# One order table for attention, RMS norm and channel mix on one core: the planner replaced, 1/rms in one pass

## The chip, the cores and the metric

The kernel runs on one core of a Trainium2 chip. Its time is the device time of one execution in microseconds; the median of several runs counts. Five engines work side by side, each through its own queue in order: TensorE (PE; its weight loads are shown apart as PEld), VectorE (DVE), ScalarE (ACT), GpSimd (POOL) and SyncE (SP). PE writes its results to PSUM, and DVE or ACT bring them to SBUF. POOL issues the loads here, SP the stores.

## What is computed

```python
# q, k, v: (8, 8, 576, 64)
kv  = einsum('bhsd,bhse->bhde', k, v)
out = einsum('bhsd,bhde->bhse', q, kv)
out = out / sqrt(mean(out * out, axis=-1) + 1e-6) * g_norm
x   = out.transpose(0, 2, 1, 3).reshape(8, 576, 512)
xp  = x shifted by one token within each batch, zero first
xk  = mu_k * x + (1 - mu_k) * xp
xr  = mu_r * x + (1 - mu_r) * xp
kk  = max(xk @ w_k, 0)                 # w_k 512 x 1024
y   = (kk * kk) @ w_v                  # w_v 1024 x 512
return sigmoid(xr @ w_r) * y           # w_r 512 x 512
```

Inputs are float32; the loads turn them into bfloat16, and the result is stored in float32.

## The kernel before

**Two halves of the work.** Attention goes by batch b (0 to 7, 576 tokens each), the channel mix by group g (0 to 8, 512 tokens each). Group g needs all batches that its tokens lie in: group 0 batch 0, group 1 batches 0 and 1, group 2 batches 1 and 2, and so on. The blended inputs lie in two rings, `xk` and `xr`, of four batches.

**Tokens and heads.** Eight heads make four head pairs (hp), and two head pairs make one z (z is 0 or 1). Features lie on the partitions and tokens on the free side. Token 9p + j stands in column 64j + p, so the shift by one token is a shift by 64 columns, with a small wrap at the edge.

**The pieces of one batch**, with their lines: `kv` (L354, 72 small matmuls) and its copy kc; `q`, the transposes of q (L362, 36 for one z), and the copy qc; `u`, which is q times kv (L369), and the copy uc (L222 on ACT, L224 on DVE); `sq`, the square on DVE (L579, L423 in batch 0); `ss`, the sum over a head by a matrix of ones (L591, L428), which leaves the sum on every partition; the logarithm of the mean plus eps on ACT (L595, L435) and the exponential of minus half of it (L599, L439), which is 1/rms; `mul`, u times 1/rms into xT on DVE (L613, L442); `wr`, the wrap (L614, L506); `d`, the difference of a token and the one before (L624, L465); `mk` and `mr`, d times a column of mu_k or mu_r, one instruction for each head pair (L638, L471); and `xk` and `xr`, that plus the token before (L641, L473). In batch 0 all of it goes in two parts of the tokens, a and b, so that group 0 can start early, and its last 64 tokens (w) come later, for group 1.

**The pieces of one group**: `k` (L692, L491 and L710 in group 0), eight pieces of four matmuls with 512 columns; `relu` on ACT (L696), one for two pieces; `ksq`, its square on DVE (L699, L716); `r`, four pieces of four (L740), and `sig` on ACT (L745); `v`, eight pieces of four (L761, L778 in the last group); `out`, v times sig on DVE (L765, L785); and the stores (L674). That makes 80 matmuls of 512 columns for a group.

**The order.** Each piece is put into a list with a set of engines that it can run on, its price, its dependencies, its buffers and a due time. `Planner.run` then plays the list through with prices of its own, takes at each step the piece that can start earliest (within a window of 0.04 us the one with the earliest due time, which counts attention from `T0 + TG * (b - 2)` and groups from `T0 + TG * g`), gives it to an engine, and emits all pieces in that order. Engines run in the order of emission. An "idle" piece of 128-column matmuls on zeros (L661) is put where PE would wait, up to a piece of batch 0.

**Buffers.** Rings hold a few tiles for each name: two each for `mm` (k, r, v) and `at` (kv, q, u, ss) in PSUM, where a tile is two banks; three for k, v and q of one batch. `qT`, `uT`, `xT`, `md` have two tiles of four head pairs, `sq`, `rs` and `d` one.

**Loads** are issued on POOL: batch 0 in pieces of 288 KB by z, then w_k in two halves of rows, w_r, w_v in one piece of 1024 KB, then each batch in three of 576 KB (q of batch 1 in two). g_norm is folded into w_k and w_r by a scaling with a column (L318). ACT changes its function table between logarithm with exponential and sigmoid (L231).

## Time and profile before

| | |
|---|---|
| median of 3 runs | 222.52 us (222.42 to 223.12) |
| the profiled execution's own time | 222.89 us |
| its span, first to last instruction | 221.1 us |
| mean granted PE clock | 0.985 |
| PE busy | 201.7 us, of which 12.7 on zeros |
| DVE, ACT, POOL busy | 145.8, 134.2, 24.2 us |
| table loads on ACT | 14, 18.0 us |
| loads and stores | 26.57 MB moved, mean 120 GB/s |

The span leaves out what lies before the first instruction and behind the last, 1.8 us here. Busy time of PE is not PE at its peak: matmuls are pipelined, so the mean of one (357 to 382 ns with 512 columns) is longer than its share of a run of them (16 take 3.45 us). A row of the groups gives line, engine, operation, output and input with shapes, count, then busy us, mean ns of one, and the idle time of the engine ahead of it with what ended it.

### The profile page before, as it was taken

Reading aid. Unit: us, or ns where it says so; the run is one execution under the profiler, and the core shown is the slowest. Engines: PE = TensorE matmul, PEld = TensorE weight load, DVE = VectorE, ACT = ScalarE, POOL = GpSimd, SP = SyncE. Lnnn points to the kernel's source line nnn. Section 1 sums busy time; section 2 is a strip of 40 time slices with the busy share of each in tenths; the row PEclk is TensorE's granted clock in tenths of the full one; section 3 lists DMA queues with packets and bytes.
Section 4 is the critical chain, followed back from the end, with each engine's and each line's share of the span. In section 5 each row is a group of like instructions: output and inputs, shape, how many; then the busy total and the mean of one; then the engine's idle time right before and its main releaser. Section 6 shows DMA issues by size and latency. Waiting matters only on the chain.

```text
span 221.1 us, 5309 instructions
## 1 busy us (share of the span) xinstructions
PE 201.7 (91%) x2260; PEld 108.0 (49%) x2285; DVE 145.8 (66%) x292; ACT 134.2 (61%) x171; POOL 24.2 (11%) x37
## 2 busy tenths in 40 slices
PE   8858779964999999999999999999999999999992
PEld 7746554443444544444345764453444444444451
DVE  1139995769995699969947993899299524224231
ACT  2236554685769987993898489749965704603610
POOL 7732124121210021000000000000000000000000
PEclk9999999996799999999999999999999999999999
DMA  5999999999999999815102500340044026007024
GB/s 81 180 210 204 208 208 207 208 241 256 206 208 208 208 233 234 150 40 128 26 0 66 127 2 3 82 110 0 3 95 96 0 47 145 0 12 181 0 68 125
DMA packets 20812, 26.57 MB, mean 120 GB/s; under 512 B 1708, under 2 KB 15796, under 8 KB 20788
## 3 DMA queue, kind: packets, MB, share of 16 engines
q0 software_dynamic: 14848, 16.78, 45.0%
q1 hardware_dynamic: 5540, 8.92, 16.2%
q10 hardware_dynamic: 400, 0.52, 0.7%
q8 instruction: 18, 0.29, 0.5%
q14 instruction: 6, 0.05, 0.1%
HBM read 33.56 MB, written 9.44 MB: 194 GB/s over the span
## 4 chain that ended last, share of the span: by engine, by line
PE 72%; DVE 10%; ACT 7%; DMA 4%; issue 4%; POOL 1%; POOLq 0%; DVEq 0%
PE mm L761 22%; PE mm L692 22%; PE mm L740 14%; DMA v<-in_v_dram 4%; PE at L591 2%; PE at L369 2%; PE at L362 2%; PE at L354 2%; PE at L778 2%; PE mm L778 2%; PE mm L710 2%; ACT relu L696 1%; DVE out L765 1%; ACT ln L595 1%; ACT uT L222 1%
## 5 line engine op out<-in xcount | busy, mean ns | idle before, releaser
L692 PE MATMUL mm<-xk,w_k 128*128 128x512 bf16 (+1 forms) x274 | 59.8, 357 | 1.2 <-issue 0.9
L696 ACT ACTIVATE relu<-mm 128x1024 bf16<-128x1024 f32 x36 | 36.8, 1025 | 39.1 <-PE mm L692 34.5
L761 PE MATMUL mm<-w_v,sqk 128*128 128x512 bf16 x248 | 57.6, 379 | 0.5 <-issue 0.2
L765 DVE TENSOR_TENSOR out<-mm,sig 128x1024 f32<-128x1024 f32 x16 | 19.6, 1223 | 33.5 <-ACT ln L595 15.4
L692 PEld LDWEIGHTS <-w_k 128*128 128x128 bf16 x288 | 26.2, 98 | 25.2 <-issue 1.1
L761 PEld LDWEIGHTS <-sqk 128*128 128x128 bf16 x256 | 24.6, 98 | 27.4 <-issue 0.5
L740 PE MATMUL mm<-w_r,xr 128*128 128x512 bf16 x141 | 32.4, 379 | 1.4 <-ACT relu L696 1.1
L699 DVE TENSOR_TENSOR sqk<-relu 128x1024 bf16<-128x1024 bf16 x32 | 21.9, 686 | 9.3 <-ACT relu L696 9.2
L740 PEld LDWEIGHTS <-xr 128*128 128x128 bf16 x144 | 13.6, 98 | 17.4 <-DVE w_r L318 1.4
L745 ACT ACTIVATE sig<-mm 128x1024 bf16<-128x1024 f32 x18 | 18.4, 1025 | 5.9 <-PE mm L740 5.7
L595 ACT ACTIVATE ln<-at,eps 128x576 f32<-128x576 f32 x28 | 19.2, 741 | 0.3 <-PE at L591 0.3
L638 DVE TENSOR_SCALAR md<-d,cols 128x576 bf16<-128x576 bf16 x56 | 18.5, 373 | 0.3
L231 ACT ACT_TABLE_LOAD x14 | 18.0, 1283 | 1.0 <-PEq L826 0.7
L599 ACT ACTIVATE rs<-ln 128x576 bf16<-128x576 f32 x28 | 17.7, 689 | 0.0
L222 ACT CAST uT<-at 128x576 bf16<-128x576 f32 (+2 forms) x24 | 13.4, 595 | 5.2 <-PE at L369 5.0
L224 DVE COPY qT<-at 128x1152 bf16<-128x1152 bf16 (+2 forms) x12 | 8.2, 682 | 10.2 <-PE at L362 10.1
L661 PE MATMUL mm<-zero 128*128 128x128 bf16 x147 | 12.7, 249 | 1.1 <-DVE zero L258 1.1
L222 ACT CAST kv<-at 128x256 bf16<-128x256 f32 (+1 forms) x9 | 3.2, 352 | 17.2 <-PE at L354 17.2
L579 DVE TENSOR_TENSOR sq<-uT 128x1152 bf16<-128x1152 bf16 x14 | 10.5, 754 | 2.9 <-PE at L591 2.5
L369 PE MATMUL at<-qT,kv 64*64 64x288 bf16 (+2 forms) x128 | 10.2, 321 | 2.0 <-ACT qT L222 1.0
L661 PEld LDWEIGHTS <-zero 128*128 128x128 bf16 x147 | 10.8, 114 | 1.9 <-DVE zero L258 1.1
L641 DVE TENSOR_TENSOR xr<-md,xT 128x1152 bf16<-128x1152 bf16 x14 | 10.6, 759 | 0.5
(58 smaller groups left out, 179.3 us busy)
## 6 DMA issues: line engine op xcount, KB each, us to landing
out_dram<-out SPq DMA_DIRECT2D x67, 128.0 KB, 2.4
k<-in_k_dram POOLq DMA_DIRECT2D x7, 576.0 KB, 20.2
v<-in_v_dram POOLq DMA_DIRECT2D x7, 576.0 KB, 21.6
q<-in_q_dram POOLq DMA_DIRECT2D x6, 576.0 KB, 21.6
q<-in_q_dram POOLq DMA_DIRECT2D x4, 288.0 KB, 15.0
w_k<-in_moe_w_k_dram POOLq DMA_DIRECT2D x2, 512.0 KB, 12.5
w_v<-in_moe_w_v_dram POOLq DMA_DIRECT2D x1, 1024.0 KB, 19.3
k<-in_k_dram POOLq DMA_DIRECT2D x2, 288.0 KB, 5.7
```

Source lines behind the costliest of these rows:

```text
L222: nc.scalar.copy(out=dst, in_=src)
L231: nc.scalar.preload_act_table_set(name)
L595: nc.scalar.activation(out=get(ln)[:, :, 0:HS], in_=ps.t[:, :, 0:HS], func=AF.Ln, bias=eps, scale=1.0 / HD)
L638: nc.vector.tensor_scalar(out=get(md)[:, hp], in0=d.t[:, hp], scalar1=cols[:, m0 + hp:m0 + hp + 1], scalar2=None, op0=ALU.mult)
L661: nc.tensor.matmul(get(k_ps[1])[:, 0, 0:128], zero[:, 0:128], zero[:, 128:256], start=not started, stop=not started)
L692: nc.tensor.matmul(get(ps)[:, fc % 2, a0:a1], w_k_sb[:, cc, 128 * fc:128 * fc + 128], xk[:, cc, x0:x0 + a1 - a0], start=(cc == 0), stop=(c ...
L696: nc.scalar.activation(out=get(rt), in_=ps.t, func=AF.Relu)
L699: nc.vector.tensor_mul(out=get(sqk)[:, 2 * f2:2 * f2 + 2, :], in0=rt.t, in1=rt.t)
L740: nc.tensor.matmul(get(ps)[:, ci % 2, :], xr[:, cc, n0:n0 + 128], w_r_sb[:, cc, :], start=(cc == 0), stop=(cc == NHP - 1))
L745: nc.scalar.activation(out=get(sg), in_=ps.t, func=AF.Sigmoid)
L761: nc.tensor.matmul(get(ps)[:, ci % 2, :], sqk.t[:, fc, 128 * ci:128 * ci + 128], w_v_sb[:, fc, :], start=(fc == 0), stop=(fc == NFC - 1))
L765: nc.vector.tensor_mul(out=get(ot)[:, xs, :], in0=ps.t[:, xs, :], in1=sg.t[:, xs, :])
```

## The change

The planner is gone. `ORDER` is a table of all pieces in the order of emission, with the engine behind an @ where there is a choice (A is ACT, D is DVE) and `z:512` for one matmul on zeros with 512 columns. `Plan.emit` runs it through. Names are as above; `sq1.01` is batch 1, z 0, second half of the tokens; `ss1.2` and `rs1.2` are batch 1, head pair 2; `v1.2.0` is group 1, 128-token chunk 2, first half of the sum; `ld` is a load, `g` a scaling of weights, `st` a store, `rs` the 1/rms pass.

Besides the order:

- 1/rms is one ACT pass (`Abs_reciprocal_sqrt`) from PSUM; the matrix of ones holds 1/64. Its function table stands in place of that of logarithm and exponential; the table is changed 12 times.
- The square can run on ACT straight from PSUM (17 of 32 do), and the column scalings `mk`, `mr` (11 of 40) and the wrap (8 of 16) can run on ACT as well.
- From batch 3 on, kv and the transposes of z 0 use one `at` tile, and the q part's copy and the kv part's copy both wait for both.
- Tiles of attention hold one z: `qT` and `uT` four, `sq` and `rs` three, `d` two, `md` four; `xT` is four constant tiles, whose zero column is set once.
- Batch 1 is loaded by z in all three inputs, w_k in halves of columns, w_v in two halves; w_k and w_r are scaled in six parts instead of three.
- In group 0, k goes in eight pieces, by half of the tokens, half of the columns of w_k, and z. A v piece waits only for the squares of its own half.
- 25 matmuls on zeros of 512 columns stand in place of 147 of 128.

The core of the diff (the first part of the table is shown to the start of group 1, then the stretch of group 2):

```diff
+ORDER = """
+ld.q0.0 small seta setb ld.v0.0 ld.k0.0 ld.q0.1 ld.k0.1 ident ld.v0.1 id9 ld.wk1 z:512 z:512 z:512 z:512 z:512 z:512
+z:512 z:512 z:512 tr9 cols ld.wk0 z:512 q0.01 ld.q1.1 q0.00 qc0.01@A qc0.00@A table ld.q1.0 z:512 z:512 z:512 z:512
+z:512 z:512 z:512 z:512 z:512 z:512 z:512 kv0.0 ld.wr kc0.0@A u0.00 u0.01 sq0.00@A uc0.00@D ld.v1.1 sq0.01@A
+uc0.01@D z:512 z:512 ss0.00 rs0.00 ss0.01 ld.k1.0 rs0.01 mul0.00 q0.10 qc0.10@D ld.k1.1 kv0.1 d0.0a q0.11 kc0.1@A
+qc0.11@D mk0.0a@A u0.10 mul0.01 u0.11 uc0.10@D sq0.10@A sq0.11@A g.wk10@D ld.v1.0 uc0.11@A ss0.10 xk0.0a rs0.10
+g.wk11@D ss0.11 k0.010 d0.0b mr0.0a@A mul0.10 d0.1a mk0.1a@A g.wk00@D ld.wv0 rs0.11 z:512 z:512 k0.000 xk0.1a
+g.wk01@D mk0.0b@A ld.wv1 mul0.11 k0.011 wr0.0@D xk0.0b d0.1b k0.001 relu0.01 ld.q2.01 mk0.1b@D q1.1 xk0.1b relu0.00
+q1.0 mr0.1b@D k0.110 d0.0w xr0.0a mk0.0w@A mr0.1a@D wr0.1@A k0.111 xr0.1a ld.k2.01 g.wr1@D k0.100 mr0.0w@D relu0.11
+ksq0.01 k0.101 g.wr0@D ld.v2.01 xr0.0w xr0.1b r0.0 mr0.0b@D relu0.10 xr0.0b ld.q3.01 r0.1 qc1.1@D qc1.0@A d0.1w r0.2
+mr0.1w@D ld.v4.01 xk0.0w ksq0.00 r0.3 ksq0.11 sig0.0 mk0.1w@D ld.k3.01 kv1 xk0.1w ksq0.10 kc1@A u1.00 u1.11 sq1.00@A
+uc1.00@D sq1.11@A ld.v3.01 uc1.11@D v0.1.0 sig0.1 u1.01 u1.10 sq1.01@A uc1.01@D v0.0.0 uc1.10@A ss1.0 ld.k4.01
+v0.1.1 sq1.10@D ss1.1 v0.0.1 rs1.0 v0.3.0 rs1.1 out0.0 ld.q4.01 ss1.3 ss1.2 rs1.3 mul1.0 v0.3.1 st0.0 rs1.2 wr1.0@D
+q2.0 d1.0 st0.1 v0.2.0 qc2.0@A mul1.1 v0.2.1 wr1.1@D mk1.0@A d1.1 q2.1 mk1.1@D ld.q5.01 mr1.0@A xk1.0 xk1.1 qc2.1@A
+kv2 out0.1 k1.0 ld.v5.01 kc2@A st0.2 u2.01 u2.00 sq2.01@A k1.1 uc2.00@D uc2.01@A ld.k5.01 k1.2 sq2.00@D relu1.0
...
+uc3.11@A v1.0.0 st0.3 mk2.0@D uc3.00@A sq3.11@D v1.0.1 sq3.00@A xk2.0 u3.10 ss3.0 sq3.10@A uc3.10@D k2.0 rs3.0
+out1.0 ss3.1 k2.1 rs3.1 st1.1 ss3.3 mul3.0 k2.2 rs3.3 mr2.0@D st1.0 wr3.0@A ss3.2 relu2.0 k2.3 xr2.0 d3.0 rs3.2
+st1.3 kv4 xr2.1 relu2.1 q4.0 ld.v7.01 q5.1 qc4.0@D k2.4 kc4@A ld.k7.01 qc5.1@A ksq2.1 k2.5 ld.q7.01 ksq2.0 ld.v6.01
+mul3.1 u4.00 relu2.2 u4.11 k2.6 wr3.1@D uc4.00@D sq4.11@A k2.7 ksq2.2 r2.2 sq4.00@D relu2.3 uc4.11@D r2.3 d3.1
...
+"""
...
+class Plan:
...
+    def emit(self, order, zeros):
+        for word in order.split():
+            if word.startswith("z:"):
+                zeros(int(word[2:]))
+                continue
+            name, _, eng = word.partition("@")
+            p = self.pieces[name]
+            eng = eng or p.on
...
+            p.fn(eng)
+            p.done = True
...
+            nc.vector.memset(ones[64 * e:64 * e + 64, 64 * e:64 * e + 64], 1.0 / HD)
...
     for i in range(2):
+        cs = slice(F // 2 * i, F // 2 * i + F // 2)
+        l = load_w(f"ld.wk{i}", w_k_sb[:, :, cs], moe_w_k[:, cs])
...
+    def rms(_, dst, ps):
+        table(RSQRT)
+        nc.scalar.activation(out=dst, in_=ps, func=AF.Abs_reciprocal_sqrt, bias=eps, scale=1.0)
...
+    def blends(b, z, name, x0, r0, w, deps, mds, dd):
...
+            def mul(eng, md=md, m0=m0):
+                for y in range(2):
+                    hp = m0 + 2 * z + y
+                    scale(eng, get(md)[:, y, cs], dd.t[:, y, cs], cols[:, hp:hp + 1])
...
+    def section(b, z, i, name, qdep, kvc, kv, qT, uT, sq, rs):
...
+        def square(eng):
+            if eng == "A":
+                nc.scalar.activation(out=get(sq)[:, :, cs], in_=us.t[:, :, 0:w], func=AF.Square)
+            else:
+                nc.vector.tensor_tensor(out=get(sq)[:, :, cs], in0=uT.t[:, :, cs], in1=uT.t[:, :, cs], op=ALU.mult)
...
+            ps0 = Buf("at")
+            m, kc = kv_piece(f"{b}", ps0 if b > 2 else Buf("at"), KC, list(range(NZ)))
...
-            a = add({"ACT": act_us(S, False, True)}, ln_act, deps=[m], bufs=[ps, ln], table="ln", name=f"ln{b}.{hp}",
-                    **when("ln", hp))
-            exps[hp] = add({"ACT": act_us(S, True)}, exp_act, deps=[a], bufs=[ln, rs], table="ln",
-                           name=f"exp{b}.{hp}", **when("exp", hp))
```

## The prediction

> **What bounds the kernel now.** I read the page's sections 1 and 2 first: which engine is full, and where it is not.

> ```profile
> span 221.1 us, 5309 instructions
> PE 201.7 (91%) x2260; PEld 108.0 (49%) x2285; DVE 145.8 (66%) x292; ACT 134.2 (61%) x171; POOL 24.2 (11%) x37
> ...
> PE   8858779964999999999999999999999999999992
> ```

> TensorE (PE) is the bound, but only from the eleventh slice on (a slice is 5.5 us). What is lost lies in the first 57 us, so I read the stages there, by windows, and the later ones for comparison. Columns: window, its length, then busy time of PE, weight loads, DVE, ACT and POOL, the granted clock, and DMA.

> ```profile
> 12.00:14.00 2.00, 0.00 (x0) 0.00 (x0) 0.93 (x5) 0.00 (x0) 0.02 (x1) 1.00 1.16 212
> ...
> 48.00:50.00 2.00, 0.60 (x45) 0.41 (x31) 1.90 (x5) 1.01 (x3) 1.48 (x2) 1.00 1.15 280
> 50.00:52.00 2.00, 0.56 (x13) 0.28 (x13) 1.97 (x4) 0.46 (x1) 0.20 (x1) 0.74 1.17 245
> 52.00:54.00 2.00, 0.80 (x12) 0.46 (x12) 1.98 (x5) 1.45 (x3) 0.54 (x1) 0.50 1.16 270
> 54.00:56.00 2.00, 1.92 (x78) 1.43 (x78) 1.98 (x4) 1.37 (x3) 0.08 (x1) 0.50 1.20 227
> ...
> 80.00:100.00 20.00, 19.50 (x171) 9.16 (x173) 17.67 (x35) 17.03 (x22) 1.56 (x3) 1.00 0.79 155
> ...
> 180.00:200.00 20.00, 19.89 (x92) 9.06 (x93) 5.78 (x7) 6.15 (x6) 0.00 (x0) 1.00 0.29 67
> ```

> At 48 to 54 us PE has almost nothing, DVE is full, and the clock falls to 0.50. From 80 us PE is full while DVE and ACT are near it (17.67 and 17.03 of 20). Then the chain of waits, to see what PE waits for at 42 to 57 us, and the groups for prices (mean ns of one):

> ```profile
> 42.53 1.28 ACT L231
> 43.82 1.37 ACT ln L595 x2
> 45.20 0.97 ACT rs L599 x2
> ...
> 49.47 1.68 issue
> ...
> 56.94 2.10 PE mm L692 x7
> ```

> ```profile
> L595 ACT ACTIVATE ln<-at,eps 128x576 f32<-128x576 f32 x28 | 19.2, 741 | 0.3 <-PE at L591 0.3
> L638 DVE TENSOR_SCALAR md<-d,cols 128x576 bf16<-128x576 bf16 x56 | 18.5, 373 | 0.3
> L599 ACT ACTIVATE rs<-ln 128x576 bf16<-128x576 f32 x28 | 17.7, 689 | 0.0
> ```

> The matmul at 56.94 is k1.0, the first of group 1. It waits for batch 1 to come through attention, normalisation and blend. Call its start K. K is what the new order can move; behind it PE is full either way.

> **From K to the end.** Before: 221.1 - 56.9 = 164.2 us. PE must do the same work behind K, except that before it had by then done u2 (about 0.6), kv3 (0.71) and half of ss2 (0.65) ahead, 2.0 us in all, which now lie behind K; and its first seven matmuls took 2.10 us at the low clock instead of 7 x 0.2156 = 1.5 (16 take 3.45 in the chain), 0.6 that goes if the clock stays up. So the new span is K + 164.2 + 2.0 - 0.6 = K + 165.6, if the stretch is as dense as now.

> **K: loads.** Landing in the trace (issue plus time to landing): the first five pieces of 288 KB at 5.4, 8.0, 9.4, 11.1 and 14.2, w_v (the tenth transfer) at 27.5. Between the last two 2,848 KB came in 13.3 us, 1.35 us per 288 KB. The new queue gives q0.0, v0.0, k0.0, q0.1, k0.1 those first five times, v0.1 15.6, wk1 18.0, wk0 20.4, q1 23.1, wr 25.5, v1.0 (last of batch 1) 30.9, w_v 33 and 36, v2 43.8. The halves of w_k have rows as short as those of w_r and w_v; priced alike, at worst 1 us more. Three more issues on POOL of 0.73 each are hidden: POOL is busy 24 of 221 us. Behind K, k3 and v3 come by 56, wanted at K + 10.

> **K: the first section.** Before, the PE queue had kv0.1 (waiting for v0.1 until 14.3) ahead of ss0.0. Now ss0.00 and ss0.01 stand ahead of q0.10 and kv0.1. kv0.0 at 9.5 or, behind eleven zeros of 0.216, up to 11; kc, u0, uc and sq (0.3 to 0.5 each) bring ss0.00 to 11.7, rs0.00 to 12.8, and d0.0a to 14.2 (before 18.96). mk0.0a stands on ACT behind kc0.1, which waits for v0.1: 16.3. q0.11, u0.10 and u0.11 bring DVE to uc0.10 at 17.4. The first k0 starts at 19 instead of 20.95.

> **K: DVE from 17.4.** From there DVE is packed. Up to ksq0.10 its queue holds, by the rows of the small shapes: 1 uc 0.49; 6 half weight scalings 2.46 (half of L318's 0.75 and 0.86); 2 mul 0.87; 3 d at 0.42 and 2 at 0.29; 8 x at 0.42 and 3 at 0.29; 4 pairs of md at 0.48 and 3 at 0.40; wrap 0.20; 4 ksq at 0.69; qc1.1 0.75: 16.7, plus 0.9 of waiting for mk0.1a on ACT. ksq0.10 ends at 35.0. Before, the last ksq ended at 34.7: up to here nothing is won, since the 1.9 us of the earlier start and the scalings given to ACT pay for work taken in. But kv1, u1.00 and u1.11 (r0.3 ends at about 32) are then done; before, kv1 began at 35.6 and u1 at 39.

> **K: batch 1.** v0.1.0 needs ksq0.10: 35.1. DVE does uc1.00, uc1.11 and uc1.01 (0.75 each) to 37.3; ACT sq1.01 and uc1.10 (0.645 each) to 37.8, a table load 1.28, and rs1.0 and rs1.1 at 0.74 to 40.5. out0.0 on DVE waits for v0.0.1 (40.0) and takes 1.22: 41.3, and mul1.0 is behind it in the queue. Then DVE alone sets the time: mul 0.75, wrap 0.20, d 0.755, the same for the other half, mk1.1 0.64, xk1.0 and xk1.1 0.76 each: 5.6, to 46.9. rs1.2 ends at 42.9, before mul1.1; mk1.0 on ACT ends behind qc2.0 (1.12) at 45.3, before xk1.0. PE's own list (v0, ss1, q2, kv2) ends at 45.5. Eight handovers of 0.05 (the "issue" pieces of the chain are 0.02 to 0.07) make K = 47.4. Compared with before, from 35 us the chain loses the four exponentials (2 x 1.25), four foreign operations among DVE's nine (qT, uT, sq, xr: about 3), and the late start of q1 and u1.

> **Sum.** 47.4 + 165.6 = 213.0 of span. The profiled execution is 222.89, 1.8 over its span: 214.8; the median of the runs is 0.4 below the profiled one: 214.4. K is uncertain by 45.5 (no wait behind out0.0) to 51 (each new handover late by 0.1, the clock low for a time).

> **Unknown prices, both ends.** The reciprocal root in one pass: same shape, source and bias column as ln, so 0.74; at least 0.645 (the PSUM copy uT), at most the pair's 1.37 (no gain). It removes 28 x 0.689 + 2.6 = 21.9 us of ACT, of which only batch 1's share lies on the path. Square from PSUM on ACT: 0.645 to 0.74; I take 0.645, the nearer row. A column scaling of 128x576 on ACT: 0.63 to 0.75 each against a DVE pair of 0.64; six full pairs and five small ones go there. ACT's total stays at about 140, DVE's at 147: the ScalarE gain is spent on moved work, so it counts only as a shorter chain. Table loads: 12 for 14; they lie beside PE. kv and the q transposes in one PSUM buffer: 0 to 1.6 saved (two waits of PE, 0.7 and 0.9, on such buffers), and below nothing if the two copies hold it longer, to -1; I take 0. Lost cover of 25 zeros for 147: 0 to 3, at 0.

> [...]

> In the rows above, 2 us of an idle PE at 12:14 left the clock at 1.00, and 1.2 us busy in 4 at 48:52 brought it down. [...]

> **Rivals.** *Denser than now* (12%): behind K only PE's sum: 8 x 80 x 0.2156 = 138.0, rest of batch 2 1.9, five batches of 0.71 + 0.82 + 0.6 + 1.3 = 3.4, tail 4.9 (matmuls end at 216.2): K + 161.9, about 210. For it: 180:200 shows 19.89 of 20. Against: cycles with attention take 21.5 (k3.0 to k4.0), not 20.7.

> *Clock or loads* (10%): PE runs at half clock in the start, or w_k's halves are late: 2 to 5 us, 217 to 220.

> *Given back later* (4%): K moves, but DVE's postponed work (xr1, out0.1, uc2: 7.8 us before r1.0, wanted at K + 8.3) makes PE starve at k2.0 by all 9: 222.5.

> *Slower* (24%): the fixed order itself. Between k1.0 and k6 PE takes pieces strictly in turn, and kv, q, u and ss share two "at" buffers, whose release hangs on ACT and DVE. By row prices the stretch from k2.0 to k3.0 holds 23.6 us on DVE against 22.6 on PE, the next 23.9 on ACT against 25.7; an order that is right for prices slightly off stalls at each late copy. It decides from (222.5 - 214.4) / 5.5 batches = 1.5 us lost for each batch more than now; at 2 it is 225. Against it: 80:100 has the same load and PE at 19.50.

> **Numbers.** My forecast, 211 to 219, has 50%. About 0.3% (0.7 us) is what a measurement of this kernel can tell from no change. Faster: 50 + 12 + 10 = 72%; same 4%; slower 24%. The range from 208 (K early and dense) to 225 (2 us a batch) leaves out some 2 in 10.

> **What would show it.** k1.0 near 47 us, with PE above 1.5 of 2 from 35 to 47 and the clock at 1.00; the first k0 matmul near 19; ACT's new pass near 0.74; cycles from k2.0 to k3.0 of at most 22. It is wrong if k1.0 is later than 51, if the slices behind 50 us show eights in PE, or if PE's waits for "at" buffers add up to more than 8 us.

## The result and the profile after

After the change the kernel takes 216.25 us (median of 4 runs, 214.56 to 217.65) against 222.82 us for the kernel before in the same session (4 runs, 222.42 to 224.14). The ratio is 0.9692, with an interval of 0.9611 to 0.9773. A second session of 6 runs gave 215.76 against 222.47, ratio 0.9704 (0.9657 to 0.9752). The profiled execution of after took 216.15 us with a span of 214.4.

The page of after, its span, engine totals, PE's slices and the granted clock:

```profile
span 214.4 us, 5046 instructions
PE 198.5 (93%) x2163; PEld 100.6 (47%) x2163; DVE 135.0 (63%) x260; ACT 136.0 (63%) x179; POOL 26.2 (12%) x40
...
PE   7966997968999999699999999999999999999991
...
PEclk9995799999999999999999999999999999999999
```

A slice is 5.4 us now. The hole that PE had in the ninth and tenth slice (6 and 4) is smaller (6 and 8). Behind the fourth slice two sixes are left: the ninth slice (43 to 48 us) and the seventeenth (86 to 91 us). The clock was low in the fourth and fifth slice. The windows say what was busy there (PE, weight loads, DVE, ACT, POOL, clock, DMA share, GB/s):

```profile
12.00:14.00 2.00, 0.98 (x11) 0.36 (x12) 0.97 (x2) 1.19 (x2) 0.71 (x1) 1.00 1.23 206
14.00:16.00 2.00, 1.27 (x49) 0.76 (x52) 1.25 (x3) 1.37 (x2) 0.71 (x1) 1.00 1.24 208
16.00:18.00 2.00, 1.28 (x59) 0.74 (x48) 1.91 (x6) 1.07 (x3) 0.71 (x1) 0.69 1.24 205
...
46.00:48.00 2.00, 0.40 (x51) 0.29 (x37) 2.00 (x5) 2.00 (x4) 0.74 (x1) 1.00 1.15 269
48.00:50.00 2.00, 0.84 (x19) 0.52 (x20) 0.82 (x1) 0.88 (x2) 0.20 (x1) 1.00 1.18 254
...
80.00:100.00 20.00, 18.20 (x244) 8.58 (x245) 15.87 (x30) 12.34 (x17) 0.00 (x0) 1.00 0.79 152
...
180.00:200.00 20.00, 20.00 (x95) 9.01 (x93) 5.89 (x8) 8.19 (x8) 0.00 (x0) 1.00 0.37 87
```

At 46 to 50 us PE was busy 1.24 of 4 us. The chain shows why (start, length, what): of kv2's 72 matmuls 56 were done when PE stopped for 2.76 us under "issue", which means that it waited for nothing that the profile shows.

```profile
45.48 0.41 PE at L290 x36
45.89 0.51 PE at L282 x56
46.40 2.76 issue
49.16 0.32 PE at L282 x16
...
87.24 1.66 issue
```

Behind that pause is K, the start of k1.0, at 49.41. Before, K was 56.94. From K to the end of the span it was 164.2 us before and is 164.9 now. So the whole gain lies before K: 7.5 us, of which 0.8 are given back.

The groups that answer to the prices of before (busy us, mean ns of one):

```profile
L302 ACT ACTIVATE rs<-at,eps 128x576 bf16<-128x576 f32 x28 | 19.9, 739 | 6.5 <-PE at L435 6.4
...
L351 ACT ACTIVATE sq<-at 128x576 bf16<-128x576 f32 x13 | 8.4, 653 | 2.9 <-PE at L297 2.9
L178 ACT ACTIVATE md<-d,cols 128x576 bf16<-128x576 bf16 x12 | 8.5, 774 | 0.0
```

The single pass took 739 ns where ln and rs took 741 and 689 one after the other.

### The profile page after: what moved, and what is told of

The parts are those of the page before. It is cut to its first block, busy times and chain, and to the rows that moved or that the text cites. A ratio compares the mean times of both kernels' runs of the same rounds, so it can differ in the third digit from the quotient of the medians.

```text
span 214.4 us, 5046 instructions
## 1 busy us (share of the span) xinstructions
PE 198.5 (93%) x2163; PEld 100.6 (47%) x2163; DVE 135.0 (63%) x260; ACT 136.0 (63%) x179; POOL 26.2 (12%) x40
## 3 DMA queue, kind: packets, MB, share of 16 engines
q1 hardware_dynamic: 5540, 8.92, 16.8%
## 4 chain that ended last, share of the span: by engine, by line
PE 86%; ACT 5%; issue 3%; DVE 2%; POOL 2%; POOLq 0%
PE mm L555 27%; PE mm L513 26%; PE mm L535 13%; PE mm L489 4%; PE at L435 3%; PE at L290 3%; PE at L297 3%; PE mm L453 2%; PE at L282 2%; PE at L555 2%; ACT sq L351 1%; DVE uT L174 1%; ACT rs L302 1%; POOL q L247 1%; ACT L188 1%
## 5 line engine op out<-in xcount | busy, mean ns | idle before, releaser
L474 ACT ACTIVATE relu<-mm 128x1024 bf16<-128x1024 f32 x36 | 36.9, 1027 | 25.5 <-PE mm L513 22.5
L513 PEld LDWEIGHTS <-w_k 128*128 128x128 bf16 x288 | 27.5, 98 | 24.5 <-issue 0.7
L523 DVE TENSOR_TENSOR sqk<-relu 128x1024 bf16<-128x1024 bf16 x32 | 21.5, 688 | 19.1 <-ACT relu L474 19.0
L568 DVE TENSOR_TENSOR out<-mm,sig 128x1024 f32<-128x1024 f32 x16 | 19.5, 1221 | 13.6 <-PE mm L555 11.7
L302 ACT ACTIVATE rs<-at,eps 128x576 bf16<-128x576 f32 (+2 forms) x32 | 22.7, 739 | 7.4 <-PE at L435 6.4
L174 DVE CAST uT<-at 128x576 bf16<-128x576 f32 (+2 forms) x15 | 11.2, 759 | 16.4 <-ACT sq L351 13.4
L180 DVE TENSOR_SCALAR md<-d,cols 128x576 bf16<-128x576 bf16 (+2 forms) x58 | 17.4, 346 | 0.3
L403 DVE TENSOR_TENSOR xT<-uT,rs 128x1152 bf16<-128x1152 bf16 (+2 forms) x18 | 12.4, 687 | 7.0 <-ACT rs L302 6.8
L314 DVE TENSOR_TENSOR d<-xT 128x1152 bf16<-128x1152 bf16 (+2 forms) x20 | 12.7, 633 | 1.1 <-ACT xT L172 0.9
L351 ACT ACTIVATE sq<-at 128x576 bf16<-128x576 f32 (+2 forms) x17 | 10.8, 652 | 4.0 <-PE at L297 3.3
L327 DVE TENSOR_TENSOR xk<-md,xT 128x1152 bf16<-128x1152 bf16 (+2 forms) x20 | 12.6, 633 | 0.6 <-ACT md L178 0.5
L178 ACT ACTIVATE md<-d,cols 128x576 bf16<-128x576 bf16 (+2 forms) x22 | 12.8, 638 | 0.2 <-DVE d L314 0.2
L172 ACT CAST uT<-at 128x576 bf16<-128x576 f32 (+1 forms) x17 | 10.4, 637 | 3.8 <-PE at L297 3.7
L327 DVE TENSOR_TENSOR xr<-md,xT 128x1152 bf16<-128x1152 bf16 (+2 forms) x20 | 12.5, 632 | 0.2
```

The source lines that it names most:

```text
L172: nc.scalar.copy(out=dst, in_=src)
L180: nc.vector.tensor_scalar(out=dst, in0=src, scalar1=col, scalar2=None, op0=ALU.mult)
L302: nc.scalar.activation(out=dst, in_=ps, func=AF.Abs_reciprocal_sqrt, bias=eps, scale=1.0)
L327: nc.vector.tensor_tensor(out=dst[:, 2 * z:2 * z + 2, r0:r0 + w], in0=md.t[:, :, cs], in1=xT[:, :, prev], op=ALU.add)
L474: nc.scalar.activation(out=get(rt), in_=ps.t, func=AF.Relu)
L513: nc.tensor.matmul(get(ps)[:, fc % 2, a0:a1], w_k_sb[:, cc, 128 * fc:128 * fc + 128], xk[:, cc, x0:x0 + a1 - a0], start=(cc == 0), stop=(c ...
```

## The experiments

Ratios are to the kernel before in the same session, with 95% intervals. K is the start of k1.0, "PE end" the last matmul's end; both are from the one profiled execution of each kernel.

| kernel | time, us | ratio | K, us | K to PE end, us |
|---|---|---|---|---|
| before | 222.3 to 222.8 | 1 | 56.94 | 160.4 |
| after, first session | 216.25 | 0.9692 (0.9611 to 0.9773) | 49.41 | 161.2 |
| after, second session | 215.76 | 0.9704 (0.9657 to 0.9752) | 48.59 | 161.4 |
| e1: new order, two passes | 224.05 | 1.0064 (1.0027 to 1.0101) | 50.70 | 168.05 |
| e2: old order, one pass | 221.99 | 0.9979 (0.9950 to 1.0007) | 55.60 | 160.95 |
| e3: moved work back on DVE | 217.71 | 0.9797 (0.9754 to 0.9840) | 48.58 | 163.6 |
| e10: loads of before | 217.77 | 0.9776 (0.9723 to 0.9829) | 51.18 | 161.9 |
| e9: own tiles for kv and first q | 220.43 | 0.9910 (0.9878 to 0.9942) | 47.84 | 166.8 |
| e4: no zeros | 212.19 | 0.9536 (0.9506 to 0.9567) | 45.85 | 160.7 |
| e5: each zero halved, one run | 219.27 | | 46.87 | 166.8 |
| e6: 13 more zeros | 217.15 | 0.9767 (0.9727 to 0.9808) | 46.20 | 165.4 |
| e7: q2.1 and half of u2 late | 217.58 | 0.9770 (0.9724 to 0.9815) | 45.53 | 164.7 |
| e8: e6 and e7 | 219.76 | 0.9877 (0.9837 to 0.9917) | 45.75 | 167.9 |
| e11: zeros of 8 columns | 214.95 | 0.9706 (0.9666 to 0.9746) | 47.68 | 161.4 |

K leans on the start as well as on the change. In after PE starts at half pace: the zeros of 512 columns begin every 0.427 us until 9.8 us and every 0.216 behind. That moment differs between executions of the same start. In e7, which differs from after only far behind it, it has come by 6.63 us, and the first k0 is at 18.85 in place of 20.17. So a K that differs by up to some 1.3 us says nothing by itself.

### After once more

> The new kernel again, on the chip and in the rounds of the three that follow, for comparison: 214.5 to 217.5.

It repeats the first result, with the stop in kv2 at 46.05 (2.29 us) and the one in r2.1 at 86.65 (1.65 us). These two stops are a property of the kernel and not of one execution.

### e1 and e2: the order and the single pass, each alone

e1 keeps the order of after and takes the root in two passes:

```
-        nc.scalar.activation(out=dst, in_=ps, func=AF.Abs_reciprocal_sqrt, bias=eps, scale=1.0)
+        ln = get(Buf("ln"))[:, :, 0:ps.shape[-1]]
+        nc.scalar.activation(out=ln, in_=ps, func=AF.Ln, bias=eps, scale=1.0)
+        nc.scalar.activation(out=dst, in_=ln, func=AF.Exp, scale=-0.5)
```

> The new kernel with 1/rms in two passes again (logarithm into a float32 tile, then exponential), the table of the order unchanged. Theory 1 (the gain is the shorter way of batch 1 to k1.0, to which the single pass gives its share): the four roots of batch 1 cost 4 x 0.63 = 2.5 us more on ACT, the first k0 is 1 us later, k1.0 moves from 49.5 to 51 to 53, and behind it little changes: 3 us slower than the new kernel, about 219. Theory 2 (the order alone, ACT has room): under 1 us, 216 to 217. Theory 3 (ACT was close to being the bound and the single pass pays all along): 20 us more on ACT cost 8 us or more, 224 or over.

e2 keeps the planner of before and gives it the single pass; the pieces "exp" fall away, and the planner sets its own order from that:

```
-  activation(out=ln_view(), in_=uq.t[:, :, 0:w], func=AF.Ln, bias=eps, scale=1.0 / HD)
-  (and exp_act behind it)
+  activation(out=get(rs)[:, hs, c0:c1], in_=uq.t[:, :, 0:w], func=AF.Abs_reciprocal_sqrt, bias=eps, scale=1.0 / HD)
```

> The kernel before with the root in a single pass and nothing else; its planner knows that there is one piece less. Theory 1: k1.0 at 56.9 comes 2.5 to 4 us earlier, behind it little changes: 218 to 220. Theory 2: no change, 222 to 223. Theory 3: the single pass brings all of it, 216 to 217.

Neither half brings the gain. e1 is 0.6% slower than before (ratio 1.0064), as the third of its theories said. K moved only from 49.41 to 50.70; the other 6.9 us that its profiled execution lost to after lie behind K. The window 110:130 of after, and then that of e1, show where:

```profile
110.00:130.00 20.00, 20.00 (x273) 12.34 (x272) 12.44 (x23) 16.81 (x23) 0.00 (x0) 1.00 0.18 41
```

```profile
110.00:130.00 20.00, 19.57 (x352) 10.41 (x352) 12.85 (x23) 18.72 (x25) 0.00 (x0) 1.00 0.18 41
```

ACT is busy 18.72 of 20 us instead of 16.81, and PE is no longer full. From 50 to 170 us PE was busy 114.20 of 120 in e1 and 118.03 in after. Two groups of e1 carry the wait in their last column:

```profile
L298 PE MATMUL at<-qT,kv 64*64 64x288 bf16 x112 | 8.3, 311 | 3.0 <-ACT ln L304 0.9 <-DVE uT L175 0.8 <-ACT kv L173 0.5
L291 PE MATMUL at<-ident,q 64*64 64x64 bf16 x576 | 8.2, 199 | 0.9 <-ACT ln L304 0.8
```

PE waits there for an "at" buffer that a ScalarE pass still reads. Behind K such waits for ln add up to 1.9 us, beside 1.4 for a copy on DVE and 0.6 for sig. Some 1.5 us more lie in the clock, which stood at 0.50 from 50.4 to 53.8 in this execution, right behind the stop in kv2 (an estimate: half of the time from K to 53.8). In the other direction, e2's ACT falls from 134.2 to 117.6 us and the time stays. But a transfer of v was late there from 49.6 to 53.5 us (PE at L354 waited 3.8 us for it, and the chain to K goes through it), in an order that the planner had made anew. What the single pass would be worth in the old order with v in time is not shown. What the two runs show is that the new order needs the single pass, and that the single pass without it gave nothing here: it frees the ACT time that the new order spends on moved scalings and squares.

### e3: the moved work back on VectorE

Every mk, mr, wr and sq of the order that was on ACT goes to DVE, sq behind its uc:

```
-  mr0.0a@A mk0.1a@A sq0.10@A wr0.1@A ...
+  mr0.0a@D mk0.1a@D sq0.10@D wr0.1@D ...
```

> The new kernel with all column scalings, squares and wraps on DVE (a square goes behind the copy that it reads); the order otherwise the same. Theory 1: in the start DVE is packed, and about 3.5 us of scalings and squares of batch 0 and 0.65 + 0.9 of batch 1 come on top, so k1.0 is 4 to 5 us later, and one stretch behind it is over PE's sum: 220 to 223. [...]

217.71, ratio 0.9797: about 2 us slower than after (0.9704 in the second session, whose interval ends where e3's begins; that of the first overlaps it), under the 220 to 223 that was expected. K is not later (48.58). DVE fills up behind it, as the windows 70:90 of after and of e3 show, but PE's busy time there is the same:

```profile
70.00:90.00 20.00, 18.03 (x339) 9.02 (x338) 18.16 (x36) 13.73 (x20) 2.23 (x3) 1.00 1.19 234
```

```profile
70.00:90.00 20.00, 17.98 (x342) 8.81 (x339) 19.39 (x38) 11.93 (x15) 2.22 (x3) 1.00 1.19 236
```

Of the 2.4 us that e3's profiled execution is longer behind K, 1.6 lie between K and the first r1 (10.18 us in place of 8.60). The clock stood at 0.50 there from 49.0 to 52.4, right behind the stop in kv2, and in after it did not:

```profile
50.00:52.00 2.00, 2.00 (x17) 0.75 (x15) 1.10 (x2) 1.25 (x3) 1.27 (x2) 1.00 1.21 209
```

```profile
50.00:52.00 2.00, 2.00 (x13) 0.74 (x13) 1.27 (x3) 0.64 (x1) 0.43 (x1) 0.50 1.25 218
```

All four executions of e3 have a mean clock of 0.966 to 0.976, seven of the ten of after 0.983 or 0.984. Whether the fuller DVE brings that about, or costs anything itself, is not shown. Up to 47.7 us DVE had 3.5 us more work than in after (27.59 against 24.14 from 17.4 us on), and K's data were ready 0.8 us later (xk1.1 ended at 48.48 for 47.69); the stop in kv2 covered that. The scaling by itself is cheaper on DVE (a pair of 128x576 at 0.65 us, one on ACT at 0.774), and the whole kernel was no faster with it there.

### e10: the loads of before

Batch 1 comes whole in each of its three inputs instead of by z, w_k in halves of its rows and w_v in one piece, much as before (where q of batch 1 came in two):

```
-  l = load_w(f"ld.wk{i}", w_k_sb[:, :, cs], moe_w_k[:, cs])
+  load_w(f"ld.wk{z}", w_k_sb[:, 2*z:2*z+2, :], moe_w_k[256*z:256*z+256, :])
+  p_wv = [load_w("ld.wv", w_v_sb, moe_w_v)] * 2
```

> The new kernel with the loads of before: batch 1 in three pieces of 576 KB, w_k in halves of rows, w_v in one piece. Theory 1 (DVE and PE set the start, not the loads): the first k0 within 0.5 us of 20.2, k1.0 within 1 us of 49.5, 215.5 to 217.5. Rival (the finer loads are what lets group 0 and batch 1 start early): w_v lands whole at about 36 instead of its first half at 33.5, v0.1.0 at 35.4 waits, k1.0 1 to 3 us later: 217 to 219.

217.77, ratio 0.9776; its interval overlaps that of after, so in the total the finer loads are worth some (0.9776 - 0.9704) x 222.5 = 1.6 us, which is not proven. In the trace they have a place: PE waited 1.9 us for w_v at v0 (to 35.57), which it does not in after, and K was 1.8 to 2.6 us later than in the two profiles of after. The clock fell with that wait, to 0.50 from 34.8 to 41.7 us. Its four executions differ: two had a mean clock of 0.958 and took 218.6 us, two had 0.976 and took 216.9.

### e9: the shared PSUM tile

kv and the first q transposes of batches 3 to 7 get tiles of their own, with the copies right behind their matmuls:

```
-  m, kc = kv_piece(f"{b}", ps0 if b > 2 else Buf("at"), KC, list(range(NZ)))
+  m, kc = kv_piece(f"{b}", Buf("at"), KC, list(range(NZ)))
   order: kc and qc.0 moved right behind kv and q for b = 3..7
```

> The new kernel with kv and the first transposes of q in tiles of their own from batch 3 on, each copy right behind its matmuls in the order. Theory 1: nothing (between 0.5 faster and 1 us slower), 216 to 217, since PE waits for at-tiles for under 1 us in all. Rival (the shared tile saves a turn of the ring for each batch): five batches at 0.5 to 1 us, 219 to 221.

220.43, in the range of the rival. But the experiment does not isolate what it was made for: the copies now stand ahead of sig in ACT's queue, and two of PE's waits are for that, beside pauses of 2.4 and 1.2 us under "issue".

```profile
PE mm L509 <- ACT sig L541: 1.7, 1, 1.7
...
PE mm L551 <- ACT sig L541: 1.4, 1, 1.4
```

What the shared tile is worth by itself stays open.

### e4, e5 and e11: the zeros and the pause

The pause in kv2 was not in the prediction. Two theories: PE waits for its next instructions, then the place depends on the number of PE instructions; or it waits for something of kv2, then the place stays. e4 drops all 25 zeros, e5 issues each as two of half the width (the same PE time, 50 more PE instructions with the weight loads), e11 keeps all 25 but with 8 columns (the same number of instructions, nearly no time):

```
e4:   -  z:512
e5:   -  z:512   +  z:256 z:256
e11:  -  z:512   +  z:8
```

> The new kernel without its 25 matmuls on zeros. Clock theory: PE starts at the low clock and stays there until the k0 matmuls have run for a while; PE is what ends the stretch from 20 to 34 us, so k0 and r0 cost 3 to 4 us more, k1.0 2 to 4 us later: 218 to 220. Rival (DVE sets the start, PE has room): within 1 us, 216. Instruction theory: 50 rows fewer ahead of kv2 move PE's pause of 2.76 us inside kv2 50 rows on, behind kv2, where matmuls are long, so that it shrinks or moves.

> The new kernel with each of the 25 matmuls on zeros of 512 columns cut into two of 256: the same PE time, 50 more instructions of PE (25 matmuls, 25 weight loads) ahead of everything. Instruction theory (PE pauses in kv2 because its next block of instructions has not come): the pause is tied to the count of instructions, so it comes 50 rows earlier, after some 31 of the 72 matmuls of kv2 instead of 56, and the one in r2.1 moves to the pieces before it. Rival (kv2 waits for data or for a port): the pause stays after the 56th. Time about the same, 216.

> The new kernel with its 25 matmuls on zeros cut from 512 columns to 8: as many instructions of PE as in the new kernel, but hardly any matmul time. It separates the two readings of the kernel without zeros (212.2). Instruction theory: the blocks of 256 rows end where they end in the new kernel, so PE pauses again inside kv2 (after row 1217) for 2.3 to 2.8 us and inside r2.1 (after row 2497) for about 1.7: 214.5 to 216.5. Rival (the time and the clock of the zeros themselves cost the 3.6 us): no pause needed, 212 to 213.

e4 is the best kernel of the study: 212.19 us (211.97 to 212.28), ratio 0.9536, clear of after's interval. PE, on the timeline, goes through kv2 without a stop, and k1.0 waits only for its own operand:

```profile
44.19 0.48 PE L287 MATMUL at<-ident,q 64*64 64x64 bf16 x36
44.77 0.77 PE L279 MATMUL at<-v,k 64*64 64x64 bf16 x72
45.85 1.26 PE L510 MATMUL mm<-xk,w_k 128*128 128x512 bf16 x4 [0.32 <-DVE xk L324]
```

The same stretch in e11, with the 50 instructions back:

```profile
44.37 0.64 PE L280 MATMUL at<-v,k 64*64 64x64 bf16 x56
47.43 0.32 PE L280 MATMUL at<-v,k 64*64 64x64 bf16 x16 [2.42 <-issue]
```

Again the stop is behind the 56th matmul of kv2, and the second one (1.65 us, in r2.1) is back too. Its ratio of 0.9706 is that of after. So the PE time of the zeros costs nothing that can be measured; their number does, by moving the places at which PE stops: 212.19 against 214.95. The forecast of the clock theory for e4, 218 to 220, did not come.

e5 has no stop in kv2, where one was expected behind the 31st matmul, and took 219.27 us where 216 was expected. Its stops are at 61.90 (3.02 us, in r1) and 82.01 (1.64 us):

```profile
64.92 1.01 PE L535 MATMUL mm<-w_r,xr 128*128 128x512 bf16 x2 [3.02 <-issue]
```

The places can be counted. Recorded instructions of PE's queue (matmuls, weight loads and some 20 of the queue itself) begun before a pause: after 1217 and 2497; e5 1729 and 2241; e11 1214 and 2487; e6 2229 and 2485; before (at 49.47 us) 1470. Divided by 256 the remainders are 193, 193, 193, 193, 190, 183, 181, 181 and 190. The smaller ones are of traces in which some matmul records are missing: with one matmul counted for each weight load, all 21 pauses of 1 us or more in the 14 traces stand at 193 or 194, whatever the matmul is. The DMA part of after's page agrees (packets, MB, share of 16 engines):

```profile
q8 instruction: 17, 0.28, 0.5%
```

17 packets of 16 KB over the 4,346 recorded PE instructions of after is one for about 256, and a part of the trace between 46.4 and 49.2 us, the pause, holds exactly one of them:

```profile
q8 instruction: 1, 0.02, 2.0%
```

So the first theory holds. The trace has the time of that packet too: it runs from 46.67 to 47.55, so it starts 0.27 us after PE has stopped, and PE goes on 1.61 us behind its end. At each of the 21 pauses PE goes on 1.2 to 1.6 us behind the end of such a packet.

How fast PE used up the block before is part of the cause. In after, the two blocks of 256 that end in a pause were used up in 3.1 and 3.9 us; those that end in none before 92 us took 5.4 or more. In e4, with 50 instructions fewer, the same two blocks by number end 50 instructions later in the program, among longer matmuls. They took 5.5 and 7.2 us, and PE did not stop behind either. In e5 the block that ends in kv2 took 6.3 us, and the expected stop is missing. That is not all of it: e1 used up a block in 4.1 us without a pause. The packet for the next one started 1.35 us behind the beginning of that block, where the two of after started 3.4 and 3.7 us behind it. Why a packet starts sooner or later stays open. All pauses lie before 92 us, while the loads keep the DMA engines full (in after share 1.16 at 46:49.2 and 1.21 at 86:89, but 0.47 at 89:100 and 0.18 at 110:130), and in or behind stretches of 64-column matmuls, which use up instructions fastest (kv's 72 in 0.77 us).

### e6, e7 and e8: the clock and the stretch of short matmuls

In after the clock fell to 0.50 from 16.8 to 23.6 us, behind the stretch with PE at 0.98 and 1.27 of 2 us. e6 adds 13 zeros in the gaps from 12.9 to 20.2 us, e7 moves the second q transpose of batch 2 and half of u2 with their copies and squares behind k1.4, e8 does both:

```
e6:  + z:512 four times before ss0.00, six times before ss0.10,
     + once each before q0.10, kv0.1 and k0.010
e7:  - q2.1 ... u2.11 u2.10 (before kv2)
     + q2.1 qc2.1@A u2.11 u2.10 uc2.11@A uc2.10@D sq2.11@D sq2.10@D (behind k1.4)
```

> The new kernel with 13 more matmuls on zeros in the gaps of PE between 12.9 and 20.2 us (4 ahead of ss0.00, 1 each ahead of q0.10, kv0.1 and k0.010, 6 ahead of ss0.10). Clock theory: the clock stays at 1.00 from 16 to 24 us, k0 and the zeros behind its first piece lose the 1.8 us that the low clock costs, kv1 at 32 instead of 33.7, k1.0 up to 1 us earlier (DVE then sets it): 0.5 to 1.8 us faster. Rival (the filling itself delays what comes): same or up to 1 us slower.

> The new kernel with q2.1, its copy and the second half of u2 moved from ahead of k1.0 to behind k1.4. Instruction theory: the block that PE waited for in kv2 (after row 1217 of its queue) then ends among the long matmuls of k1, the pause of 2.76 us goes, k1.0 starts at 47.7 when xk1.1 is done: 1 to 1.7 us faster if batch 2 is not late for it, since its second half comes 5 us later. Rival (the pause has another cause, or batch 2 becomes late): no gain, up to 2 us slower at k2.0.

> Both of the two before: 13 more matmuls on zeros, q2.1 late. If both hold, 1.5 to 3 us faster than the new kernel, 212.5 to 215. But 26 more rows of PE move the block's end 26 rows earlier, into the end of kv2 or just behind it, so that part of the pause may come back.

All three were expected to gain, 0.5 to 1.8 us, 1 to 1.7 and 1.5 to 3. None did. e6's and e7's intervals overlap that of the same session's after, e8's lies clear above it, so it is slower. Each reached what it was made for. e6's clock stayed at 1.00:

```profile
16.00:18.00 2.00, 1.75 (x11) 0.83 (x12) 1.62 (x4) 1.38 (x3) 0.42 (x1) 1.00 1.25 208
```

K came at 46.20, 2.4 us before that of the same session's after. This is not the clock alone: e6 has no pause in kv2 either, since its 26 instructions move the places, and waits 1.7 us for ACT (md) there instead. Behind K PE lost it by two pauses and a wait for ACT (sig):

```profile
PE at L296 <- issue: 1.9, 1, 1.9
PE at L281 <- ACT md L177: 1.7, 1, 1.7
PE at L289 <- issue: 1.6, 1, 1.6
PE at L281 <- ACT sig L544: 1.6, 1, 1.6
```

e7 had K at 45.53, no pause in kv2, and a new wait of 1.2 us for the copy that it moved (qT), beside a pause of 1.65. e8 had both gains before K (45.75) and the largest loss of the three behind it (167.9): two pauses of 1.6 us, the wait for qT, and the clock at 0.50 from 53.8 to 57.2 right behind that wait. An earlier K is not yet a shorter kernel: the fixed order behind it was made for other times.

## Why the prediction was right, and where it was not

The forecast was 214.4 us, the measurement 216.25; faster, as the likeliest case said.

**From K to the end** was forecast at 165.6 and measured at 164.9. The step holds, but with a term that it did not have: a stop of 1.66 us in r2.1 at 87.24. So the closeness of the sum is in part luck: without the stop it is 163.3. The cycle from k2.0 to k3.0, which holds the stop, took 25.9 us where at most 22 were set as its mark (k1.0 to k2.0: 22.4). Of the signs of being wrong, low slices behind 50 us did show, as the six at 86 to 91 us.

**K** was forecast at 47.4 and came at 49.41. Its data came 0.8 us late: xk1.1 ended at 47.69 (forecast 46.9), which the timeline shows. The other 1.7 us lie behind that.

```profile
46.27 1.42 DVE L327 TENSOR_TENSOR xk<-md,xT 128x1152 bf16<-128x1152 bf16 x2
```

The step that failed is "PE's own list ends at 45.5": with the 2.76 us of the stop, which no term of the sum held, it ended at 49.4. One such stop was in the shown chain of before (1.68 us of "issue" at 49.47) and was read past. In e4, where it is absent, K is 45.85 and the time 212.19.

**The first section**: the first k0 came at 20.17, forecast 19. The failed term is the eleven zeros, priced at 0.216 each. Here are after's, then e7's (ten are recorded):

```profile
7.27 3.85 PE L453 MATMUL mm<-zero 128*128 128x512 bf16 x11
```

```profile
6.63 2.55 PE L451 MATMUL mm<-zero 128*128 128x512 bf16 x10
```

In after most of them ran at half pace, so kv0.0, queued behind them, began at 11.05, the upper end that the prediction gave and did not use, and the chain behind it slid. In e7, with the same start, PE was at full pace by 6.63 us: kv0.0 waited for k until 9.72, and the first k0 came at 18.85, as forecast. So the step is right for one execution and wrong for another. The list up to ksq0.10 (forecast 35.0, measured 34.27) and batch 1's chain (out0.0 ended 42.28 for 41.3; mul1.0 began at 42.20, right behind it, as said) were near.

**VectorE as what sets K** holds for the last stretch. From out0.0 at 41.06 to the end of xk1.1 at 47.69 DVE works without a gap, and in e4, without the pause, k1.0 waits for xk (0.32 us). From 17.4 to 35 us it is not shown: the chain of after goes through the matmuls of k0 and q1 (20.38 to 30.29) and then through ACT (relu, qT, table load, sig, kv to 34.95). From 24 to 34 us PE was busy 10.00 of 10 us and DVE 9.79, and e3's 3.5 us of more DVE work made K's data only 0.8 us later. Both engines are near full there. (The six half weight scalings add up to 2.36 by their rows, not 2.46.)

**The prices**: single pass 0.74, measured 0.739; Square 0.645, measured 0.653; column scaling on ACT 0.63 to 0.75, measured 0.774 for the full shape, above its range. ACT's total came to 136.0 instead of about 140, DVE's to 135.0 instead of 147. "The ScalarE gain counts only as a shorter chain" was wrong: e1, without it, lost 6.9 us behind K, where ACT's passes hold PE up.

**Lost cover of the zeros**, priced at 0 to 3 and taken as 0: no run shows the 3. What after shows is that the clock did fall, from 16.8 to 23.6, and that k0's first eight matmuls took 1.91 us in place of about 0.9. This is the rival "clock or loads", in part. From the first k0 at 20.17 to 23.6 half pace costs some 1.7 us (an estimate from these times), under the 2 to 5 of the rival. e6, with the clock at 1.00, does not price it cleanly, as said above. The zeros did not help either. Without any (e4) k0's matmuls of 256 columns began every 0.213 us until 22.7 and every 0.109 behind; in after full pace came at 9.8 us, among the zeros, but it was lost again from 16.8 to 23.6. So both are at full pace at about the same time. Ahead of the fall at 16.8 PE was busy 2.25 of the 4 us from 12 to 16, and its longest idle stretch between the first kv and the fall was 1.02 us (to 13.91). Which measure of PE's work counts is not shown.

**The slower rival**, an order that stalls at each late copy, is what e1 shows (ratio 1.0064, PE short of full by 5.8 us from 50 to 170): with ACT at 18.72 of 20 in the window shown it costs, at 16.81 it does not. The rival "denser than now", K + 161.9, did not come: of the kernels with the new order e4 is the nearest, with K + 164.5.

## What to carry to other kernels

An engine with spare time and a cheaper step for it belong together: the single pass alone gave nothing here, the order that used its room alone lost, and both gave 3%. When PE stops under "issue" with no semaphore named, count its instructions to that point and see whether the count falls on a fixed step; removing 50 useless ones was worth more here than any further change of the order tried. A fixed order has to be judged at its end: e5, e6, e7, e8 and e9 all had K earlier by over 1.5 us than the first profile of after and a longer stretch behind it, and none took less time.

## What the runs showed of the hardware

A stop can cost twice. In e3 the granted clock stood at 0.50 for 3.4 us right behind the stop of 2.39 us in kv2, and in after, behind one of 2.76 us, it did not.

In after and e4 PE starts at half pace, and the granted clock of the views does not show it. In e4 the matmuls of 256 columns begin every 0.213 us until 22.7 us and every 0.109 behind. The trace's first clock record lies at 22.71, and the views show the time ahead of it as 1.00. In after the first record lies at 9.95, where the zeros go from 0.427 to 0.216 us.
